# The sign of a 64-bit weight comes in with its scaling: windowed attention and two expert layers on one core

## Chip, cores and metric

One core of a Trainium2 chip. The metric is the device time of one execution in microseconds (us), as the median of several runs; the profile comes from one execution of its own.

## What is computed

Three stages follow one another: a windowed causal attention (4 sequences, 8 heads, 576 positions, 64 columns per head, window 128), an expert layer with a rational function, and an expert layer with an exponential unit. Cut to what matters:

```python
scores = where(mask, scale * q @ k.T - slope * abs(rel), -1e9)
x  = softmax(scores) @ v                       # 2304 tokens x 512
h  = x @ w_in                                  # 512 x 2048
g  = (a0 + a1*h + a2*h**2 + a3*h**3) / (1 + abs(b0)*abs(h) + abs(b1)*h**2 + 1e-6)
x  = g @ w_out                                 # 2048 x 512
h  = x @ w2_in
g  = where(h > 0, h, exp(min(h, 0)) - 1)
out = g @ w2_out
```

All four weight matrices arrive as 64-bit floats. The kernel makes 32-bit values of them on the chip, and splits each of these into a rounded part (type fp32r) and a rest, so that three matmuls of fp32r parts stand for one of full precision.

## The kernel before

**One weight word.** A 64-bit float lies in memory as a low and a high 32-bit word. Read as a 32-bit float, the high word has the right order of exponent bits, but three bits too far to the right. The kernel converts a tile of 128x512 words in four steps, named by letters: `s` (`conv_scale`, L126) multiplies the high words by 2^-112; `a` (`conv_shift`, L141) shifts the low words right by 29; `b` (`conv_or`, L144) shifts the scaled words left by 3, which pushes the sign out, and sets the three bits of `a`; `c` (`conv_sign`, L151) takes the sign bit of the high word by an "and" and sets it by an "or". Then `h` (`conv_hi`, L158) writes the rounded part over the place of the raw words, and `l` (`conv_lo`, L166) the rest. `s` writes into one of three rotating tiles (`cvt`), so the `s` of a tile waits until the `l` of the third tile before it has read.

**Attention.** 16 units (a sequence and a pair of heads) run as a software pipeline. Each iteration of its loop goes through the list `STEPS` (L18), which fixes by hand the order of the work on each engine; the number beside a step says of which unit, ahead or behind, it is the step. `T` are transposes of probabilities on TensorE, `C` their copies out of PSUM, `S` the scores, `D` the shifted scores with their maximum (VectorE, L503), `E` the exponentials with their sums (ScalarE, L518; each ends with a read of the accumulator), `R0` and `R1` the inverses of the sums (VectorE, L527 and L530), `N` the scaling of the probabilities by them (GpSimd, L535), `V` and `Y` the products with v, `XC` the copy of the result (ScalarE, L444, tile `xT`). `PLAN` (L32) puts the conversion of two weight tiles, numbered 0 and 1, into each of 12 units: steps `s0`, `s1`, `a0` and so on. `ENG` (L37) names the engine of a step: `s0` runs on GpSimd, `s1` on ScalarE, `h0` and `h1` on ScalarE, the rest of the conversion on VectorE. The order on the engines that matters below, within one iteration:

- ScalarE: `C01`, `C00`, `E6`, `E8`, `C10`, `C11`, `E1`, `E2`, `E4`, `E3`, `s1`, `E0`, `h1`, `E7`, `qC`, `h0`, `E5`, `XC`
- VectorE: `a0`, `l1`, `a1`, `D1`, `D3`, `l0`, `D2`, `D4`, `R1`, `b0`, `D0`, `kC`, `c0`, `D7`, `D5`, `D6`, `R0`, `b1`, `D8`, `c1`, `zC`, `XY`

Eight more tiles are converted around the end of the attention and in the first block of the rational layer by `conv_step` (L181), in the same steps.

**Rational layer.** 96 steps of 12 matmuls into `h` (L260) and 12 into `acc` (L708) alternate on TensorE; ScalarE and VectorE compute the rational function between them. Beside 54 of these steps half a tile of the next layer's weights is converted (`join_scale` on ScalarE, `join_shift`, `join_words`, `join_sign` on VectorE) and stored to DRAM by a transfer from the SP queue.

**Exponential layer.** A planner (`in_order`, L1127) puts all steps in order from a cost and a due time of each. Five weight tiles are still converted here (`scale_wo`, `join_wo`), with a planned cost of 1600 ns for the VectorE part.

Of the kernel before, what the change touches and what calls it, by code (L numbers as in the profile page):

```python
# [9 lines left out]
F32 = mybir.dt.float32  # L10
F32R = mybir.dt.float32r
I32 = mybir.dt.int32
# [24 lines left out]
ENG = {  # L37
    "h0": "A", "h1": "A", "s0": "G", "s1": "A", "l0": "D", "l1": "D", "qC": "A", "kC": "D",
    "zC": "D", "XC": "A", "XY": "D", "C00": "A", "C01": "A", "C10": "A", "C11": "A",
# [5 lines left out]
def kernel(  # L45
# [79 lines left out]

    def conv_scale(key, eng="A"):  # L126
        T32[key] = t = cv_tile([P, PC], F32, "cvt")
        high = words(key)[1].bitcast(F32)
        if eng == "G":
            nc.gpsimd.tensor_scalar(  # L130
                out=t, in0=high, scalar1=2.0 ** -112, scalar2=1.0, op0=ALU.mult, op1=ALU.mult
            )
        else:
            nc.scalar.activation(out=t, in_=high, func=AF.Copy, scale=2.0 ** -112)  # L134

# [8 lines left out]
    def conv_or(key):  # L144
        low, _ = words(key)
        ti = T32[key].bitcast(I32)
        nc.vector.scalar_tensor_tensor(
            out=ti, in0=ti, scalar=3, in1=low, op0=ALU.logical_shift_left, op1=ALU.bitwise_or
        )

    def conv_sign(key):  # L151
        _, high = words(key)
        ti = T32[key].bitcast(I32)
        nc.vector.scalar_tensor_tensor(
            out=ti, in0=high, scalar=-2147483648, in1=ti, op0=ALU.bitwise_and, op1=ALU.bitwise_or
        )
# [24 lines left out]
    def conv_step(keys, more=True, later=False):  # L181
        while put_off:
            go_on()
        if not (keys or stage["scaled"] or stage["whole"]):
            return
        new = keys.pop(0) if keys and more else None
        scaled, whole = stage["scaled"], stage["whole"]
        stage["scaled"], stage["whole"] = new, scaled
        if whole:
            conv_hi(whole)  # L190
        if new:
            conv_scale(new)
        if scaled:
            put_off.append(lambda: conv_shift(scaled))
            put_off.append(lambda: conv_or(scaled))
            put_off.append(lambda: conv_sign(scaled))
        if whole:
            put_off.append(lambda: conv_lo(whole, "D"))
        while put_off and not later:
            go_on()  # L200
# [124 lines left out]
    def attention():  # L325
        with ExitStack() as es:
# [280 lines left out]
            for e in range(2):  # L607
                RUN[f"V{e}"] = attn_v(e * NF // 2)
                for half in range(2):
                    RUN[f"T{e}{half}"] = probs_T(e, half)  # L610
                    RUN[f"C{e}{half}"] = probs_T_copy(e, half, ENG[f"C{e}{half}"])
            CONV = {"s": conv_scale, "a": conv_shift, "b": conv_or, "c": conv_sign, "h": conv_hi, "l": conv_lo}

# [82 lines left out]
    def experts():  # L696
# [71 lines left out]
        def join_scale(n):  # L768
            if n >= 2 * len(early_ones):
                return  # L770
            high = half[n].rearrange("p (c t) -> p c t", t=2)[:, :, 1]
            whole[n] = w = row("glo3" if n % 2 else "ghi3")[:, 0:HC]
            nc.scalar.activation(out=w, in_=high.bitcast(F32), func=AF.Copy, scale=2.0 ** -112)

# [9 lines left out]

        def join_sign(n):
            high = half.pop(n).rearrange("p (c t) -> p c t", t=2)[:, :, 1]
            w = whole.pop(n)
            wi = w.bitcast(I32)
            nc.vector.scalar_tensor_tensor(
                out=wi, in0=high, scalar=-2147483648, in1=wi, op0=ALU.bitwise_and, op1=ALU.bitwise_or  # L790
            )
            key = early_ones[n // 2]
            if n % 2 == 0:
                joined[key] = dram.tile([P, PC], F32, name="joined_%s_%d" % key)
            nc.sync.dma_start(out=joined[key][:, n % 2 * HC:(n % 2 + 1) * HC], in_=w)
# [27 lines left out]
        def scale_wo(q, e):  # L823
            key = ("wo", KF + 2 * q + e)
            T32[key] = both(e)
            nc.scalar.activation(out=both(e), in_=words(key)[1].bitcast(F32), func=AF.Copy, scale=2.0 ** -112)

        def join_wo(q, e):
            key = ("wo", KF + 2 * q + e)
            conv_shift(key)  # L830
            conv_or(key)
            conv_sign(key)
            del RAW[key]
# [204 lines left out]
        def weight_steps(w):  # L1038
# [22 lines left out]
            for e, x in enumerate("EF"):  # L1061
                gone = [(w - 2, "G", n) for n in ((0, 3), (1, 2))[e]]
                if e in raw_ones(w):
                    if w > 0:
                        step((w, "raw", x), "SP", 600, lambda e=e: load_raw(w, e), *gone)
                    step((w, "scale", x), "ACT", 570, lambda e=e: scale_wo(w, e), (w, "raw", x), (w - 1, "lo", x),
                         (w - 1, "keep", x))
                    step((w, "words", x), "DVE", 1600, lambda e=e: join_wo(w, e), (w, "scale", x))
                    step((w, "keep", x), "SP", 600, lambda e=e: keep_wo(w, e), (w, "words", x))
# [156 lines left out]
        for s in range(NCH):  # L1226
# [10 lines left out]
            if joins(s):  # L1237
                rational(s, beside=(lambda: join_shift(nj), lambda: join_words(nj), lambda: join_sign(nj)))
                nj += 1
# [50 lines left out]
```

## Time and profile before

| | |
|---|---|
| time, median of 3 runs | 941.23 us (939.8 to 941.63) |
| the profiled execution, first to last instruction | 939.7 us |
| busy: TensorE, VectorE, ScalarE, GpSimd | 920.0, 815.8, 745.7, 199.7 us |
| instructions | 16811 |

The span runs from the first to the last instruction of the program; the runs' times also hold what lies around it. In the rows below, PE is TensorE, PEld its weight loads, ACT is ScalarE, DVE is VectorE, POOL is GpSimd. An instruction of ACT or DVE can begin before the one ahead of it has ended, so its cost in a full queue is the distance between two starts, which is less than its duration. Shares of the whole span are averages over three stages with different limits.

### The profile page before, as it was taken

The page shows a single profiled execution, that of the slowest core. Times are in us where ns is not written, and L with a number is a line of the kernel's source. Part 1 is how long each engine was busy: PE and PEld are TensorE (multiplying, and loading weights), DVE is VectorE, ACT ScalarE, POOL GpSimd, SP SyncE. Part 2 cuts the span into 40 slices and gives each one's busy share as a digit, 9 for nine tenths or more (in the row PEclk, how much of TensorE's full clock was granted, in tenths as well). Part 3 has the DMA queues.
Part 4 walks back from the last instruction along what each step waited for, and adds up shares of the span by engine and source line. Part 5 has one row for each costly group of instructions (what it writes and reads, how often), then busy time and mean ns, then how long its engine had stood idle before and what let it go on. Part 6 is the DMA issues. An engine that isn't in the chain of part 4 may idle for free.

```text
span 939.7 us, 16811 instructions
## 1 busy us (share of the span) xinstructions
PE 920.0 (98%) x5494; PEld 840.3 (89%) x5494; DVE 815.8 (87%) x1930; ACT 745.7 (79%) x1635; POOL 199.7 (21%) x272
## 2 busy tenths in 40 slices
PE   8999989999999999999999999999999999999998
PEld 5776768999999999999999998888888888888887
DVE  6999998999999999999999999999968688777653
ACT  6999998889889889889888987576867567766553
POOL 5777772122222222222222220000000000000000
PEclk9999999999999999999999999999999999999999
DMA  9899942011231222222211043444353422442201
GB/s 192 226 227 229 235 129 90 1 34 35 85 98 55 85 84 68 84 70 85 80 45 34 1 135 112 149 145 159 109 169 113 123 79 90 157 146 80 79 0 68
DMA packets 112423, 98.35 MB, mean 105 GB/s; under 512 B 62800, under 2 KB 86096, under 8 KB 112336
## 3 DMA queue, kind: packets, MB, share of 16 engines
q1 hardware_dynamic: 109936, 96.70, 35.3%
q10 hardware_dynamic: 2400, 0.59, 0.4%
q8 instruction: 43, 0.70, 0.3%
q14 instruction: 44, 0.36, 0.1%
HBM read 79.96 MB, written 17.30 MB: 103 GB/s over the span
## 4 chain that ended last, share of the span: by engine, by line
PE 70%; ACT 13%; DVE 13%; issue 2%; DMA 1%; DVEq 0%; ACTq 0%; SPq 0%
PE acc L937 21%; PE m L921 18%; PE h L260 14%; PE acc L708 14%; ACT pT L444 2%; ACT pr_wi L518 2%; ACT pr_wo L518 2%; DVE ghi L301 2%; DVE qq L304 2%; DVE ee L322 1%; DVE ee L318 1%; DVE qq L313 1%; DVE h L321 1%; ACT cvt L134 1%; DMA k_wi<-in_k_dram 1%
## 5 line engine op out<-in xcount | busy, mean ns | idle before, releaser
L260 PE MATMUL h<-xs,w_wi 128*128 128x384 f32 x1152 | 218.2, 335 | 1.3 <-ACT xs L235 0.8
L260 PEld LDWEIGHTS h<-xs,w_wi 128*128 128x128 f32 x1152 | 200.5, 188 | 4.2 <-DVE xs L236 2.4
L708 PE MATMUL acc<-ghi,w_wo 128*128 128x384 f32 x768 | 194.9, 334 | 0.0
L319 POOL TENSOR_TENSOR glo<-ee,rr 128x384 fp32r<-128x384 f32 x92 | 93.4, 1015 | 316.4 <-DVE ee L318 161.0
L708 PEld LDWEIGHTS acc<-ghi,w_wo 128*128 128x128 f32 x768 | 138.6, 188 | 0.0
L708 PE MATMUL acc<-glo,w_wo 128*128 128x384 f32 x384 | 128.6, 335 | 0.4 <-POOL glo L319 0.2
L307 ACT ACTIVATE rr<-qq,c_q 128x384 f32<-128x384 f32 x96 | 59.2, 617 | 39.1 <-DVE qq L304 38.1
L937 PE MATMUL acc<-op_wo,ghi 128*128 128x512 f32 x288 | 89.6, 392 | 0.0
L921 PE MATMUL m<-xo_wo,op_wi 128*128 128x384 f32 x336 | 77.5, 339 | 2.3 <-DVE ee L977 2.3
L921 PE MATMUL m<-xo_wi,op_wi 128*128 128x384 f32 x336 | 77.8, 339 | 0.0
L708 PEld LDWEIGHTS acc<-glo,w_wo 128*128 128x128 f32 x384 | 72.1, 188 | 1.2 <-POOL glo L319 1.2
L290 ACT ACTIVATE oo<-h,a_sb 128x384 f32<-128x384 f32 x96 | 67.9, 707 | 4.4 <-DVE h L321 3.7
L983 ACT ACTIVATE oo<-qq 128x384 f32<-128x384 f32 x24 | 12.6, 525 | 72.7 <-DVE qq L977 72.7
L293 ACT ACTIVATE ee<-h,a_sb 128x384 f32<-128x384 f32 x96 | 67.6, 704 | 0.0
L921 PEld LDWEIGHTS m<-xo_wo,op_wi 128*128 128x128 f32 x336 | 61.6, 190 | 6.4 <-ACT oo L987 2.6
L301 DVE TENSOR_TENSOR ghi<-ee,rr 128x384 fp32r<-128x384 f32 x96 | 53.6, 559 | 12.2 <-ACT oo L290 0.5
L322 DVE TENSOR_TENSOR ee<-ee,h 128x384 f32<-128x384 f32 x96 | 53.3, 555 | 10.0
L937 PEld LDWEIGHTS acc<-op_wo,ghi 128*128 128x128 f32 x288 | 53.5, 188 | 8.9
L921 PEld LDWEIGHTS m<-xo_wi,op_wi 128*128 128x128 f32 x336 | 61.1, 189 | 0.0
L304 DVE SCALAR_TENSOR_TENSOR qq<-h,b_abs,qa 128x384 f32<-128x384 f32 x92 | 55.9, 608 | 3.7 <-ACT qa L289 3.7
L977 DVE TENSOR_TENSOR ee<-ee,m 128x384 f32<-128x384 f32 x96 | 52.6, 549 | 5.1 <-PE m L921 4.9
L937 PE MATMUL acc<-op_wo,glo 128*128 128x512 f32 x144 | 56.9, 395 | 0.0
(197 smaller groups left out, 2125.4 us busy)
## 6 DMA issues: line engine op xcount, KB each, us to landing
pair<-joined_wo SPq DMA_DIRECT2D x43, 256.0 KB, 2.7
raw_wo<-in_moe_w_out_dram SPq DMA_DIRECT2D x20, 512.0 KB, 5.1
raw_wi<-in_moe_w_in_dram SPq DMA_DIRECT2D x16, 512.0 KB, 4.5
half<-in_moe_w_in_dram SPq DMA_DIRECT2D x32, 256.0 KB, 2.8
two_wo<-joined_wi SPq DMA_DIRECT2D x32, 256.0 KB, 3.0
s<-sums SPq DMA_DIRECT2D x32, 256.0 KB, 2.8
half<-in_moe_w_out_dram SPq DMA_DIRECT2D x22, 256.0 KB, 2.8
v<-in_v_dram SPq DMA_DIRECT2D x32, 128.0 KB, 3.3
```

The costliest lines, as they stand in the source:

```text
L260: nc.tensor.matmul(h, lhsT=WT["wi", f][:, SEL[wp], kk * P:(kk + 1) * P], rhs=x[xp][kk], start=(kk == 0 and n == 0), stop=(kk == KD - 1 and ...
L290: nc.scalar.activation(out=oo, in_=h2, func=AF.Identity, scale=a_sb[:, 3:4], bias=a_sb[:, 1:2])
L293: nc.scalar.activation(out=ee, in_=h2, func=AF.Identity, scale=a_sb[:, 2:3], bias=a_sb[:, 0:1])
L301: nc.vector.tensor_tensor(out=hi, in0=ee0, in1=rr0, op=ALU.mult)
L304: nc.vector.scalar_tensor_tensor(out=qq, in0=h2, scalar=b_abs[:, 1:2], in1=qa, op0=ALU.mult, op1=ALU.add)
L307: nc.scalar.activation(out=rr, in_=qq, func=AF.Ln, bias=c_q)
L319: (nc.gpsimd if c > 4 else nc.vector).tensor_tensor(out=low, in0=ee0, in1=rr0, op=ALU.mult)
L322: nc.vector.tensor_tensor(out=ee, in0=ee, in1=h, op=ALU.add)
L708: nc.tensor.matmul(acc_t[d], lhsT=WT["wo", f][:, SEL[wp], d * P:(d + 1) * P], rhs=gt[SEL[xp]], start=(f == 0 and n == 0), stop=(f == KF - ...
L921: nc.tensor.matmul(out, lhsT=w[:, SEL[wp], c0:c0 + P], rhs=XO[q // NP2, nm, k][:, SEL[xp]], start=(k == 0 and n == 0), stop=(k == 1 and n ...
L937: nc.tensor.matmul(acc_t[T, t], lhsT=gt[SEL[xp]][:, t * P:(t + 1) * P], rhs=w[:, SEL[wp]], start=(first and n == 0), stop=(last and n == 2),)
L977: nc.vector.tensor_tensor(out=t, in0=R[q, x], in1=M[q, m], op=ALU.add)
```

## The change

The scaling becomes a Prelu, which multiplies a positive value by 1 and a negative one by a slope. With scale 2^-112 and slope 2^32, a negative value keeps one more exponent bit, which the shift left by 3 moves into the place of the sign. Step `c` goes away everywhere: 24 tiles in the attention, 8 by `conv_step`, 54 half tiles in the rational layer, 5 tiles in the exponential layer. In the attention `s0` moves from GpSimd to ScalarE, and `h0` and `h1` move from ScalarE to VectorE, at the same places of `STEPS`. The planner counts 950 ns in place of 1600 for the VectorE part of the last five tiles.

```diff
-    ("c0", 1), ("D7", 1), ("E4", 1), ("N7", 0), ("N8", 0), ("D5", 1), ("E3", 1),
+    ("D7", 1), ("E4", 1), ("N7", 0), ("N8", 0), ("D5", 1), ("E3", 1),
...
-    ("qT", 3), ("h1", 0), ("b1", 1), ("D8", 1), ("V1", -1), ("E7", 1), ("c1", 1),
+    ("qT", 3), ("h1", 0), ("b1", 1), ("D8", 1), ("V1", -1), ("E7", 1), 
...
-    "h0": "A", "h1": "A", "s0": "G", "s1": "A", "l0": "D", "l1": "D", "qC": "A", "kC": "D",
+    "h0": "D", "h1": "D", "l0": "D", "l1": "D", "qC": "A", "kC": "D",
...
+    def scale_words(out, high):
+
+        nc.scalar.activation(out=out, in_=high, func=AF.Prelu, scale=2.0 ** -112, alpha=2.0 ** 32)
...
-    def conv_sign(key):
-        _, high = words(key)
-        ti = T32[key].bitcast(I32)
-        nc.vector.scalar_tensor_tensor(
-            out=ti, in0=high, scalar=-2147483648, in1=ti, op0=ALU.bitwise_and, op1=ALU.bitwise_or
-        )
...
-            put_off.append(lambda: conv_sign(scaled))
...
-            nc.scalar.activation(out=w, in_=high.bitcast(F32), func=AF.Copy, scale=2.0 ** -112)
+            scale_words(w, high.bitcast(F32))
...
-                    step((w, "words", x), "DVE", 1600, lambda e=e: join_wo(w, e), (w, "scale", x))
+                    step((w, "words", x), "DVE", 950, lambda e=e: join_wo(w, e), (w, "scale", x))
...
-                rational(s, beside=(lambda: join_shift(nj), lambda: join_words(nj), lambda: join_sign(nj)))
+                rational(s, beside=(lambda: join_shift(nj), lambda: join_words(nj), lambda: keep_half(nj)))
```

`conv_scale` and `scale_wo` call `scale_words` too; `keep_half` is what was left of `join_sign`: the transfer to DRAM.

## Rows read from the trace of the kernel before

**Rows 1.** Stretch, length, busy PE, PEld, DVE, ACT, POOL, clock, DMA share, GB/s.
```profile
50.00:120.00 70.00, 66.61 (x663) 48.97 (x660) 69.46 (x266) 70.00 (x219) 54.27 (x81) 1.00 0.91 226
156.00:560.00 404.00, 402.55 (x2308) 399.47 (x2308) 376.12 (x810) 353.78 (x697) 93.36 (x92) 1.00 0.20 60
570.00:925.00 355.00, 355.00 (x1765) 319.51 (x1764) 283.73 (x559) 232.58 (x469) 0.00 (x0) 1.00 0.36 112
```

**Rows 2.** Chain that ended last, 82 to 120 us, shares by engine and line.
```profile
by line: ACT pT L444 21.8%; ACT pr_wo L518 20.2%; ACT pr_wi L518 16.6%; issue 14.0%; ACT cvt L134 7.6%; ACT rr L518 5.5%; ACT w_wi L164 5.3%; ACT qkT L444 5.1%; ACT w_wo L164 4.2%
```

**Rows 3.** ScalarE in order of time: start us, duration us, what; two iterations' ends.
```profile
35.86 0.58 ACT L444 ACTIVATE xT<-x 128x512 f32<-128x512 f32 x1
...
122.57 0.58 ACT L444 ACTIVATE xT<-x 128x512 f32<-128x512 f32 x1
```

**Rows 4.** ScalarE in order of time, one iteration: E8, s1, E0, h1, E7.
```profile
63.79 0.55 ACT L518 ACTIVATE pr_wo<-pr_wo,qq 128x256 f32<-128x256 f32 x1
...
66.99 0.73 ACT L134 ACTIVATE cvt<-raw_wo 128x512 f32<-128x512 f32 x1
67.56 0.50 ACT L518 ACTIVATE rr<-rr,qq 128x192 f32<-128x192 f32 x1
67.91 0.25 ACT L518 ACTIVATION_READ_ACCUMULATOR rr<-rr,qq 128x1 f32 x1
68.00 0.68 ACT L164 ACTIVATE w_wo<-cvt 128x512 fp32r<-128x512 f32 x1
68.52 0.55 ACT L518 ACTIVATE pr_wi<-pr_wi,qq 128x256 f32<-128x256 f32 x1
```

**Rows 5.** VectorE in order of time: R0, c1, zC, a0, l1.
```profile
60.28 0.24 DVE L527 TENSOR_SCALAR qq<-qq 128x5 f32<-128x5 f32 x1
...
61.57 0.69 DVE L154 SCALAR_TENSOR_TENSOR cvt<-raw_wo,cvt 128x512 int32<-128x512 int32 x1
62.17 0.28 DVE L446 COPY qkT<-ty 128x128 f32<-128x128 f32 x1
...
62.51 0.42 DVE L137 TENSOR_SCALAR raw_wi<-raw_wi 128x512 int32<-128x512 int32 x1
62.84 0.68 DVE L168 TENSOR_TENSOR w_wo<-cvt,w_wo 128x512 fp32r<-128x512 f32 x1
```

**Rows 6.** GpSimd in order of time: s0 and what it waited for.
```profile
63.61 0.79 POOL L130 TENSOR_SCALAR cvt<-raw_wi 128x512 f32<-128x512 f32 x1 [1.15 <-DVE w_wo L168]
```

**Rows 7.** VectorE groups by shape: busy us, mean ns of one, idle before them.
```profile
L446 DVE COPY qkT<-ps_qk 128x512 f32<-128x512 f32 x16 | 11.0, 685 | 0.0
L137 DVE TENSOR_SCALAR raw_wo<-raw_wo 128x512 int32<-128x512 int32 x20 | 8.4, 422 | 0.0
L789 DVE SCALAR_TENSOR_TENSOR glo<-half,glo 128x256 int32<-128x256 int32 x27 | 11.3, 418 | 0.0
```

**Rows 8.** ScalarE groups: busy us, mean ns of one, idle before them.
```profile
L307 ACT ACTIVATE rr<-qq,c_q 128x384 f32<-128x384 f32 x96 | 59.2, 617 | 39.1 <-DVE qq L304 38.1
L308 ACT ACTIVATE rr<-rr 128x384 f32<-128x384 f32 x96 | 50.5, 526 | 3.0
L638 ACT ACT_TABLE_LOAD x1 | 1.3, 1283 | 2.7 <-issue 2.7
```

**Rows 9.** ScalarE in order of time behind the attention's last conversions.
```profile
144.65 0.63 ACT L164 ACTIVATE w_wi<-cvt 128x512 fp32r<-128x512 f32 x1 [0.52 <-DVE cvt L154]
```

**Rows 10.** Chain that ended last, 160 to 214 us, shares by engine and line.
```profile
by line: DVE ghi L301 12.3%; DVE qq L304 11.8%; DVE ee L318 7.7%; DVE ee L322 7.4%; DVE h L321 7.2%; DVE qq L313 7.0%; ACT rr L307 5.6%; ACT oo L290 5.1%; ACT rr L308 4.9%; DVE cvt L154 4.5%; DVE cvt L147 4.5%; issue 3.8%; ACT cvt L134 3.5%
```

**Rows 11.** Waits of TensorE, 190 to 220 us: us in total, times, longest.
```profile
PE h L260 <- ACT xs L235: 0.5, 1, 0.5
PE h L260 <- DVE xs L236: 0.4, 1, 0.4
```

**Rows 12.** Wait of TensorE, 540 to 600 us.
```profile
PE m L921 <- DVE ee L977: 2.3, 1, 2.3
```

**Rows 13.** Chain that ended last, 478 to 565 us, shares by engine and line.
```profile
by line: DVE ghi L301 10.7%; DVE ee L322 9.8%; DVE qq L304 9.2%; DVE ee L318 7.8%; DVE qq L313 7.7%; DVE h L321 6.7%; issue 6.6%; ACT rr L307 3.5%; DVE xo_wi L878 3.3%; ACT rr L308 3.0%; DVE xo_wo L878 2.9%; DVE s L851 2.5%; ACT h L288 2.4%
```

More of the change, by code (lines that the diff above doesn't have):

```diff
@@ L124, in words, with conv_scale @@
         return raw[:, :, 0], raw[:, :, 1]
-    def conv_scale(key, eng="A"):
+    def scale_words(out, high):
+        nc.scalar.activation(out=out, in_=high, func=AF.Prelu, scale=2.0 ** -112, alpha=2.0 ** 32)
+    def conv_scale(key):
         T32[key] = t = cv_tile([P, PC], F32, "cvt")
         high = words(key)[1].bitcast(F32)
-        if eng == "G":
-            nc.gpsimd.tensor_scalar(
-                out=t, in0=high, scalar1=2.0 ** -112, scalar2=1.0, op0=ALU.mult, op1=ALU.mult
-            )
-        else:
-            nc.scalar.activation(out=t, in_=high, func=AF.Copy, scale=2.0 ** -112)
+        scale_words(t, high)
     def shift(low):
@@ L148, in conv_or @@
             out=ti, in0=ti, scalar=3, in1=low, op0=ALU.logical_shift_left, op1=ALU.bitwise_or
-        )
-    def conv_sign(key):
-        _, high = words(key)
-        ti = T32[key].bitcast(I32)
-        nc.vector.scalar_tensor_tensor(
-            out=ti, in0=high, scalar=-2147483648, in1=ti, op0=ALU.bitwise_and, op1=ALU.bitwise_or
         )
@@ L611, in attention @@
                     RUN[f"C{e}{half}"] = probs_T_copy(e, half, ENG[f"C{e}{half}"])
-            CONV = {"s": conv_scale, "a": conv_shift, "b": conv_or, "c": conv_sign, "h": conv_hi, "l": conv_lo}
+            CONV = {"s": conv_scale, "a": conv_shift, "b": conv_or, "h": conv_hi, "l": conv_lo}
             def run(step, u):
@@ L783, in join_words, with keep_half @@
             )
-        def join_sign(n):
-            high = half.pop(n).rearrange("p (c t) -> p c t", t=2)[:, :, 1]
+        def keep_half(n):
+            half.pop(n)
             w = whole.pop(n)
[L788 to L791, printed above, removed]
             key = early_ones[n // 2]
@@ L825, in scale_wo @@
             T32[key] = both(e)
-            nc.scalar.activation(out=both(e), in_=words(key)[1].bitcast(F32), func=AF.Copy, scale=2.0 ** -112)
+            scale_words(both(e), words(key)[1].bitcast(F32))
         def join_wo(q, e):
@@ L831, in join_wo @@
             conv_or(key)
-            conv_sign(key)
             del RAW[key]
```

## The prediction, made before the changed kernel was run

> **What bounds the kernel now.** I read the busy time by stage first, because the whole-span shares mix three stages. From 156 us to 560 us, the rational layer, TensorE is busy 402.55 of 404 us, and from 570 to 925 us, the exponential layer, 355.00 of 355 [rows 1]. There the other engines have room: ScalarE is busy 353.78 of 404 and 232.58 of 355. What the change takes off VectorE and ScalarE in these two stages is worth nothing, except at the few places where TensorE stands still. The attention is different: from 50 to 120 us ScalarE is busy 70.00 of 70 us and VectorE 69.46, TensorE 66.61 [rows 1]. The chain of waits in this stage has ScalarE instructions alone, and among them the scaling (7.6%) and the rounded parts (5.3% and 4.2%) that the change moves [rows 2]. So the change is worth what it takes off an iteration of the attention, times the iterations, and what it takes off TensorE's stalls later. When the attention ends earlier, all that follows begins earlier, since TensorE is full from there on.
>
> One iteration lasts (122.57 - 35.86) / 10 = 8.67 us, the copy `XC` from the one to the other ten iterations later [rows 3].
>
> **The attention, engine by engine.** On ScalarE the two `h` go: one costs 68.52 - 68.00 = 0.52 us from start to start, two 1.04. `s0` comes in, at the price of `s1`, 67.56 - 66.99 = 0.57 [rows 4]. ScalarE by itself would need 8.67 - 1.04 + 0.57 = 8.20 us. On VectorE the two `c` go, 62.17 - 61.57 = 0.60 each, and two copies of 128x512 from SBUF to SBUF come [rows 5]. No such copy stands in the trace. A bound from below is the shift, one input, the same size, both sides in SBUF: 422 ns long, and 62.84 - 62.51 = 0.33 from start to start [rows 5, 7]. A bound from above is a copy of the same size out of PSUM, 685 ns long, or `l1`, as long as `c`, so 0.60 from start to start [rows 5, 7]. I take 0.33, since the shift shares with the copy both the single input and the place of its data. The Trainium skill, "VectorE: DVE Perf Modes", section on the perf-mode tier table, says that 32-bit copies and tensor-scalar operations within SBUF run at two elements per cycle and that PSUM operands lose this; 422 against 685 ns agrees, and by that rule the copy comes out at the lower price too. VectorE by itself then needs 8.67 - 1.20 + 0.66 = 8.13 us. GpSimd loses `s0` (0.79 us) and the 1.15 us for which it stood in front of it [rows 6]; it was not on the chain, so this counts as nothing.
>
> **A new wait.** Neither 8.20 nor 8.13 is what I expect, because `s0` brings its wait along. GpSimd waited 1.15 us with it for `l1` [rows 6]: `s0` needs the rotating tile that `l1` frees. On ScalarE everything queues behind that wait, `E8` to `E0`, and `R0` on VectorE waits for `E0`, and `l1` comes behind `R0`. This is a ring through both engines, and its length is a lower limit of the iteration. ScalarE from `E8` to `E0`: 67.56 - 63.79 = 3.77, plus 0.57 for `s0`. `E0` with its accumulator read: 67.91 + 0.25 - 67.56 = 0.60 [rows 4]. VectorE from the start of `R0` to the end of `l1`: 62.84 + 0.68 - 60.28 = 3.24, less `c1` 0.60, plus the two copies 0.66 (both stand between `R0` and `l1`) = 3.30 [rows 5]. For each of the two passages from engine to engine 0.09, as `l1` ended at 63.52 and `s0` began at 63.61 [rows 5, 6]. The sum is 4.34 + 0.60 + 3.30 + 0.18 = 8.42 us. The ring is longer than either engine's own work, so it sets the iteration: 0.25 us less than now, in 12 iterations **3.0 us**. Before the change there was no such ring, as `s0` stood in a queue of its own.
>
> The price of the Prelu is the other unknown. From below it is that of the Copy that it replaces. From above: an operand that is read per partition costs 617 - 526 = 0.09 us more here, for two functions of otherwise equal size [rows 8]; if the slope were read so, `s0` and `s1` would each be dearer by 0.09. I take the lower, since scale and slope are both constants in the code.
>
> **The end of the attention.** One more `h` (0.52 us) leaves ScalarE in the iteration after the twelve. Behind it ScalarE stood 0.52 us for a sign step in front of a rounded part [rows 9]; in this `conv_step` the sign goes and the wait with it. Both lie on the chain that leads to TensorE's full stretch: **1.0 us**.
>
> **TensorE's stalls in the rational layer.** Between 156 and 560 us TensorE is idle for 404 - 402.55 = 1.45 us [rows 1], of which 0.9 us are waits for the split of the next block near 214 us [rows 11]. The chain up to there runs through VectorE, and sign steps are 4.5% of its 54 us, that is 2.4 us in four steps [rows 10]. This is more than the stalls are, so nearly all of them should go: **1.0 us**, between 0 and 1.3.
>
> **The change of layers.** Near 565 us TensorE waits 2.3 us for VectorE [rows 12], and the chain runs back through VectorE and ScalarE to 478 us [rows 13]. From 478 us on, three of the `join_sign` are left out, each 0.34 us from start to start (418 ns long [rows 7], with the overlap of 0.08 of the longer ones). That is 1.0 us if VectorE keeps the lead until 565 us and 0 if it only waits longer for TensorE in between: **0.5 us**.
>
> **What costs nothing.** The other 51 `join_sign` (0.34 us each, 17 us of VectorE) lie under TensorE's full queue, and so do the five `c` of the exponential layer; the planner's new cost can reorder steps there, under the same cover. If that cover were gone, a misplaced step would show as a wait of TensorE, of which there are none now between 570 and 925 us [rows 1]. The transfers behind `keep_half` stay at their place. The transfers of weights and of q, k and v come closer together in the attention (DMA share 0.91 there [rows 1]); an iteration 3% shorter asks for 3% more, and their first users come iterations later, so I count nothing.
>
> **Sum.** 3.0 + 1.0 + 1.0 + 0.5 = 5.5 us off the profiled span of 939.7 us. The median of the runs, 941.23, is 1.5 us above that span (what lies around it, and the scatter of runs); I take the difference off the median: 935.7 us.
>
> **Rivals.**
>
> - *The ring is not felt*, because VectorE reaches `l1` earlier than I think. Then ScalarE's own 8.20 us holds: 0.47 x 12 = 5.6 us, in all 8.1 off, 933.1 us; with all stalls gone 932.3. For it: ScalarE waits for nothing in this stage now. Against it: the ring's parts are all measured, and `E0` does stand in front of `R0`.
> - *The slope is read like a per-partition operand.* The ring is 8.60, the gain 0.07 x 12 = 0.8, in all 3.3 off: 937.9 us.
> - *The copy runs at the upper price*, 0.60 from start to start. The ring grows to 8.42 + 0.54 = 8.96 us, which is 0.29 more than now: 12 iterations lose 3.5 us, the other terms give 2.5 back, 942.2 us. With a copy above 0.46 us the attention becomes slower than it is. If the slope is dearer besides, 944.3.
> - *The Prelu is not in the table that is loaded*, so the change doesn't do what it says. The trace has one table load in all, of 1283 ns [rows 8], for every function used. A load in front of each scaling and one behind it would be 2.57 us. In the attention this is 24 x 2.57 = 62 us on the engine that is full. In the rational layer ScalarE is idle (404 - 353.78) us over the 96 steps of that layer, 0.52 per step, so each of 54 joins would cost 2.05 us, 111 in all: 941 + 173 - 5.5, about 1109 us. It decides as soon as the function is missing. The Trainium skill, "ScalarE: Activation LUTs", section on table sets, says that functions are loaded in named sets, that cheap functions are in every set, and that each switch of sets is paid; it names no Prelu in its list, and no row here has one. What speaks against this rival in the trace is that six different functions run behind the one load.
>
> **How the numbers follow.** Chances: the forecast 0.45, the ring not felt 0.15, the dearer slope 0.17, the dearer copy 0.13, the missing table entry 0.05, and 0.05 for a wait that I don't see and that eats the gain. 0.2% is 1.9 us, about what a measurement of this kernel can tell from no change. Faster by more: 0.45 + 0.15 + 0.17 = 0.77. Within it: most of the dearer copy and of the unseen wait, 0.12. Slower: the table, and the dearer copy with the dearer slope, 0.11. The forecast alone lies between 934 and 938 us. The range reaches from 932.3 (everything gained) to 940.5, which leaves out the dearer copy and the table.
>
> **What the profile after would show.** The distance of the `XC` copies should be 8.4 us, with ScalarE idle some 0.2 us in each iteration in front of `s0`, released by `l1`, and VectorE idle in front of `R0`. The copies on VectorE should last 0.42 us, the Prelu as long as the Copy before, 0.67 to 0.73. TensorE's waits near 214 us should be gone and the one near 565 us shorter. The prediction is wrong if the copies last 0.68, if there is more than one table load, or if the iteration is shorter than 8.3 us.

## The result, and the profile after

The changed kernel takes 933.23 us, median of 4 runs (933.09 to 933.9), against 941.05 us for the kernel before in the same session (4 runs, 939.8 to 941.63). The ratio is 0.9919, interval 0.9905 to 0.9933. The forecast was 935.7 us in a range of 932.3 to 940.5: the time is in the range, and the gain is 7.8 us where 5.5 were forecast. The profiled execution after took 933.09 us with a span of 931.4, which is 8.3 us shorter than the span before. Part of the 7.8 us is TensorE's clock, which fell to its lower level for 3.4 us at a time in some executions (below). Among the runs with a mean granted clock of 1.00, 17 of the kernel before have a median of 939.4 us, and the two of the changed kernel took 933.13 (here) and 932.1 (e13): about 6.8 us at equal clock.

Busy time by stage after, in the columns of [rows 1]:

```profile
50.00:120.00 70.00, 68.33 (x696) 51.16 (x697) 68.94 (x273) 69.07 (x218) 46.44 (x76) 1.00 0.95 228
150.00:550.00 400.00, 399.24 (x2299) 398.32 (x2300) 361.00 (x750) 354.49 (x697) 93.67 (x92) 1.00 0.19 61
560.00:917.00 357.00, 357.00 (x1772) 321.16 (x1772) 282.63 (x557) 233.49 (x470) 0.00 (x0) 1.00 0.34 112
```

In the attention VectorE (68.94) and ScalarE (69.07) are still nearly full, and TensorE has come up to 68.33. Later, TensorE is full as before.

ScalarE after, in order of time: two ends of an iteration, ten iterations apart [rows 3], and between them one turn of the ring [rows 4]. L128 is the scaling `s0` (it reads `raw_wi`), L509 with `rr` is `E0`:

```profile
34.62 0.59 ACT L435 ACTIVATE xT<-x 128x512 f32<-128x512 f32 x1
...
62.12 0.70 ACT L128 ACTIVATE cvt<-raw_wi 128x512 f32<-128x512 f32 x1
...
66.51 0.44 ACT L509 ACTIVATE rr<-rr,qq 128x192 f32<-128x192 f32 x1
66.86 0.19 ACT L509 ACTIVATION_READ_ACCUMULATOR rr<-rr,qq 128x1 f32 x1
...
70.24 0.19 ACT L509 ACTIVATION_READ_ACCUMULATOR pr_wo<-pr_wo,qq 128x1 f32 x1
70.55 0.70 ACT L128 ACTIVATE cvt<-raw_wi 128x512 f32<-128x512 f32 x1
...
119.03 0.58 ACT L435 ACTIVATE xT<-x 128x512 f32<-128x512 f32 x1
```

An iteration lasts (119.03 - 34.62) / 10 = 8.44 us, against 8.67 before; the forecast was 8.42. Ahead of the second `s0`, ScalarE stands idle from about 70.33 (a read of the accumulator costs 0.09 from start to start) to 70.55: 0.22 us, the wait that the prediction expected there.

VectorE in the same iteration [rows 5]: `R0` (L518), the new copies `h1` and `h0` (L154, listed as CAST), `a0` (L136, `raw_wi`), `l1` (L160, `w_wo`), `a1` (L136, `raw_wo`) and the step behind it:

```profile
67.07 0.32 DVE L518 TENSOR_SCALAR qq<-qq 128x5 f32<-128x5 f32 x1
67.43 0.19 DVE L521 RECIPROCAL qq<-qq 128x5 f32<-128x5 f32 x1
67.54 0.39 DVE L154 CAST w_wo<-cvt 128x512 fp32r<-128x512 f32 x1
67.84 0.69 DVE L146 SCALAR_TENSOR_TENSOR cvt<-cvt,raw_wo 128x512 int32<-128x512 int32 x1
...
68.99 0.42 DVE L154 CAST w_wi<-cvt 128x512 fp32r<-128x512 f32 x1
69.32 0.22 DVE L437 COPY xT<-ty 128x64 f32<-128x64 f32 x1
69.45 0.48 DVE L136 TENSOR_SCALAR raw_wi<-raw_wi 128x512 int32<-128x512 int32 x1
69.85 0.67 DVE L160 TENSOR_TENSOR w_wo<-cvt,w_wo 128x512 fp32r<-128x512 f32 x1
70.44 0.63 DVE L136 TENSOR_SCALAR raw_wo<-raw_wo 128x512 int32<-128x512 int32 x1
70.99 0.27 DVE L494 CUSTOM_DVE_ANT_0 pr_wi<-s_ps,h 128x128 f32<-128x128 f32 x1
```

The copies cost 67.84 - 67.54 = 0.30 and 69.32 - 68.99 = 0.33, as forecast. But the shifts have grown: `a1` costs 70.99 - 70.44 = 0.55 and `a0` 69.85 - 69.45 = 0.40, where a shift cost 0.33 before, and `R0` costs 67.43 - 67.07 = 0.36, where it cost 0.27 (60.55 - 60.28 in the trace before). No idle time stands in front of `R0`, where the prediction expected some. GpSimd beside it [rows 6]:

```profile
66.44 0.93 POOL L526 TENSOR_SCALAR pr_wo<-pr_wo,qq 128x256 f32<-128x256 f32 x2
...
69.62 1.16 POOL L526 TENSOR_SCALAR pr_wi<-pr_wi,qq 128x256 f32<-128x256 f32 x1
```

Its work ends at 66.44 + 0.93 = 67.37, and `R0` ends at 67.39. Its instruction from 69.62 ends at 70.78, and `a1`, begun at 70.44, lets the next step start 0.21 us after that. `s0` has left GpSimd, and its other work now falls beside these steps. In the kernel before `R0` ended at 60.52 [rows 5], and GpSimd beside it at 60.49:

```profile
60.02 0.47 POOL L535 TENSOR_SCALAR pr_wo<-pr_wo,qq 128x256 f32<-128x256 f32 x1
```

So `R0` already ended with a GpSimd instruction there, 0.07 us later than where it is free (0.17 long in e10).

Groups over the whole span (busy us, mean ns of one, idle before) [rows 7, 8]:

```profile
L154 DVE CAST w_wi<-cvt 128x512 fp32r<-128x512 f32 x12 | 5.0, 418 | 0.0
L136 DVE TENSOR_SCALAR raw_wo<-raw_wo 128x512 int32<-128x512 int32 x20 | 10.5, 527 | 0.0
L128 ACT ACTIVATE cvt<-raw_wi 128x512 f32<-128x512 f32 x16 | 11.1, 693 | 0.8
L629 ACT ACT_TABLE_LOAD x1 | 1.3, 1283 | 2.7 <-issue 2.7
```

There is one table load, as before. The Prelu lasts 693 ns, in the band that was given for it (0.67 to 0.73). The copy lasts 418 ns, and the shift has gone from 422 to 527 in the mean.

TensorE's waits from 140 to 560 us [rows 11, 12]:

```profile
PE m L907 <- DVE ee L963: 2.3, 1, 2.3
PE ps_pT L542 <- ACT pT L435: 1.4, 1, 1.4
```

The waits for `xs` near 214 us are gone. The wait at the change of layers is 2.3 us, as before.

From the two traces, between instructions that both have:

| stretch | before | after | gained | forecast |
|---|---|---|---|---|
| start to the first `XC` copy | 27.11 | 26.06 | 1.05 | 0 |
| twelve iterations of the attention, 1st to 13th `XC` | 103.68 | 100.93 | 2.75 | 3.0 |
| end of the attention, to TensorE's `h` at 162.14 (157.05 after) | 31.35 | 30.06 | 1.29 | 1.0 |
| first block of the rational layer, to `acc` at 216.66 (209.29) | 54.52 | 52.24 | 2.28 | 1.0 with the next row |
| the other blocks, to `acc` at 551.09 (542.62) | 334.43 | 333.33 | 1.10 | |
| change of layers and exponential layer, to the last `m` | 374.33 | 374.48 | -0.15 | 0.5 |

The rest to the end is 14.3 us in both. The sum is 8.3 us.

In the first and the third row the two executions differ in TensorE's clock, too, and in the last row it fell in both. The kernel before, in three stretches (columns as above):

```profile
16.00:18.00 2.00, 2.00 (x12) 1.23 (x9) 1.49 (x7) 1.93 (x10) 1.28 (x3) 0.50 0.67 154
151.60:155.00 3.40, 3.40 (x28) 3.00 (x28) 2.85 (x6) 3.16 (x8) 0.00 (x0) 0.50 0.49 158
564.70:567.90 3.20, 2.94 (x9) 2.97 (x10) 2.72 (x6) 2.29 (x6) 0.00 (x0) 0.50 0.29 76
```

The changed kernel at the start and behind the change of layers:

```profile
16.00:18.00 2.00, 1.93 (x16) 1.32 (x15) 1.97 (x12) 2.00 (x9) 1.41 (x4) 1.00 0.74 162
557.50:560.50 3.00, 3.00 (x10) 2.91 (x10) 1.85 (x4) 2.77 (x7) 0.00 (x0) 0.50 0.00 1
```

And a second execution of the changed kernel (e13) behind the change of layers:

```profile
557.50:560.50 3.00, 3.00 (x17) 2.78 (x16) 3.00 (x6) 3.00 (x8) 0.00 (x0) 1.00 0.06 23
```

The granted clock was 0.50, the lower of its two levels, three times in that execution of the kernel before, once in that of the changed kernel, and never from the start to the end of e13. The later falls came at the end of a stop of TensorE or within 0.9 us behind it: 2.1 us long until 151.23 in the kernel before, 2.3 us at the change of layers in both. The same stop of 2.2 to 2.3 us stands in all 14 profiled executions, and the clock fell there in five of them: before, after, e1, e5 and e10. What each fall cost:

- Start: the first `XC` comes at 25.7 to 26.6 us in the other profiles (26.02 in e13), except in e6 (27.36, where TensorE waits for q), so about 1 us of the first row belongs to that execution of the kernel before. This is inferred, not tested.
- End of the attention: the last interval of `XC` is 8.00 us before and 7.64 to 7.66 in every other profile, with and without sign steps. So 0.35 of the 1.29 us is the clock, and 0.94 the change.
- Exponential layer: the last row takes 374.3 to 374.5 us where the clock fell (before, after, e5), 372.9 in e13. The fall costs 1.5 us, and it hits both kernels of the table alike.

### The profile page after: what moved, and what is told of

Read it like the earlier page. It is cut to its first block, busy times and chain, and to the rows that moved or that the text cites. A ratio compares the mean times of both kernels' runs of the same rounds, so it can differ in the third digit from the quotient of the medians.

```text
span 931.4 us, 16710 instructions
## 1 busy us (share of the span) xinstructions
PE 913.8 (98%) x5494; PEld 838.8 (90%) x5494; DVE 792.0 (85%) x1863; ACT 741.9 (80%) x1623; POOL 185.2 (20%) x260
## 4 chain that ended last, share of the span: by engine, by line
PE 79%; DVE 14%; ACT 3%; DMA 2%; issue 1%; DVEq 0%; ACTq 0%; SPq 0%
PE acc L923 21%; PE m L907 18%; PE acc L699 18%; PE h L251 18%; DVE pr_wi L494 2%; DVE pr_wo L494 1%; DVE cvt L146 1%; PE s_ps L468 1%; DVE qkT L437 1%; DVE ghi L292 1%; PE x L561 1%; DVE ee L313 1%; DMA q_wo<-in_q_dram 1%; PE ps_pT L542 1%; DVE w_wi L160 1%
## 5 line engine op out<-in xcount | busy, mean ns | idle before, releaser
L279 ACT ACTIVATE h<-h 128x384 f32<-128x384 f32 x96 | 46.3, 483 | 14.8 <-PE h L251 14.2
```

## The experiments

All but e6 are edits of the changed kernel, e6 is one of the kernel before. Their ratios are to the kernel before on the same chip, with which they alternated (the medians of the kernel before: 940.25 us beside e1 to e4, 940.88 beside e6, e7, e9 and e10, 939.52 beside e5 and e11 to e13).

**e1, open the ring.** `s0` goes behind `C10` in `STEPS`, so that ScalarE has `l1`'s release before it gets there.

```diff
-    ... ("T10", -1), ("s0", 1), ("D1", 1), ...
+    ... ("T10", -1), ("D1", 1), ...
-    ... ("R1", 0), ("b0", 1), ...
+    ... ("R1", 0), ("s0", 1), ("b0", 1), ...
```

> The changed kernel with the scaling of tile 0 (s0) put after C10 in the list of steps, so that ScalarE reaches it long after l1 has freed its tile; nothing else differs. Theory (the ring s0, E0, R0, l1 sets the iteration of 8.44 us): the ring shrinks by E8 and C10, about 0.97 us, so it no longer sets the end; the iteration falls to ScalarE's own 8.20 to 8.25 us, ScalarE no longer waits in front of s0, and the time is 12 x 0.2 = 2.4 us under the changed kernel's 933.2: 930.8. Rival (the iteration is set by something else, VectorE held up by GpSimd or TensorE): the iteration stays within 0.05 of 8.44 us and the time within 0.6 of 933.2.

Measured: 933.52 us, 0.9925 (0.9903 to 0.9947), the same as the changed kernel. The steady iteration stays at 8.43 to 8.45 us, so the rival holds. `R0` now begins 0.26 us after the end of `E0` (0.02 in the changed kernel), and `s0` 0.76 us after `l1` (0.03): the ring is open. VectorE and GpSimd of e1 in order of time:

```profile
75.10 1.39 POOL L526 TENSOR_SCALAR pr_wo<-pr_wo,qq 128x256 f32<-128x256 f32 x3
...
76.15 0.37 DVE L518 TENSOR_SCALAR qq<-qq 128x5 f32<-128x5 f32 x1
...
79.56 0.63 DVE L136 TENSOR_SCALAR raw_wo<-raw_wo 128x512 int32<-128x512 int32 x1
```

`R0` again ends with GpSimd's work (76.52 and 76.49), `a1` is as long as in the changed kernel, and VectorE has no idle time from 60 to 118 us. So the ring is not alone in setting 8.44: with it open, VectorE by itself is just as long.

**e10, the shift `a1` behind `D3`**, where GpSimd has finished; `s0` stays in its place.

```diff
-    ("a1", 1), ("E6", 0), ("T10", -1), ("s0", 1), ("D1", 1), ("D3", 1), ("E8", 0),
+    ("E6", 0), ("T10", -1), ("s0", 1), ("D1", 1), ("D3", 1), ("a1", 1), ("E8", 0),
```

> The changed kernel with only the shift a1 moved behind D3; s0 stays where the change has it. It tells whether the ring through ScalarE is a limit of its own at 8.4 us beside VectorE's work, since a1 does not lie between R0 and l1. If the ring is a limit: the iteration stays at 8.4 to 8.44 us, VectorE stands idle about 0.2 us in front of R0 in each iteration and ScalarE in front of s0, 933 us. If VectorE's work alone is one: 8.23 us and 931, as with both steps moved.

Measured: 931.42 us, 0.9902 (0.9887 to 0.9917); the iteration is 8.26 to 8.29 us. VectorE of e10 in order of time, `R0`, `l1` and `a1`:

```profile
66.65 0.17 DVE L518 TENSOR_SCALAR qq<-qq 128x5 f32<-128x5 f32 x1 [0.16 <-ACT rr L509]
...
69.27 0.67 DVE L160 TENSOR_TENSOR w_wo<-cvt,w_wo 128x512 fp32r<-128x512 f32 x1
...
70.42 0.42 DVE L136 TENSOR_SCALAR raw_wo<-raw_wo 128x512 int32<-128x512 int32 x1
70.75 0.68 DVE L160 TENSOR_TENSOR w_wi<-cvt,w_wi 128x512 fp32r<-128x512 f32 x1
```

`a1` is back at 70.75 - 70.42 = 0.33, `R0` at 0.17 long, and now VectorE does wait 0.16 us for `E0`. This is the ring of the prediction, at 8.28 us. Neither expectation came whole: the idle time in front of `R0` is there, as for a ring that is the limit, but the ring is shorter than 8.4, since `R0` now begins 0.10 us before GpSimd's work ends and costs 0.20 (66.85 - 66.65) in place of 0.36. The stretch from `R0` to the end of `l1` is 69.27 + 0.67 - 66.65 = 3.29 us (3.30 forecast).

**e9, both moves together.**

```diff
-    ("a1", 1), ("E6", 0), ("T10", -1), ("s0", 1), ("D1", 1), ("D3", 1), ("E8", 0),
+    ("E6", 0), ("T10", -1), ("D1", 1), ("D3", 1), ("a1", 1), ("E8", 0),
-    ... ("R1", 0), ("b0", 1), ...
+    ... ("R1", 0), ("s0", 1), ("b0", 1), ...
```

> The changed kernel with two steps moved in the list: s0 behind C10 (as in the run before this one, which opened the ring and left the iteration at 8.44 us) and the shift a1 behind D3, a place at which GpSimd is idle. Theory now (VectorE's own work is the limit, and it is 0.3 us longer than I added up, because a1 takes 0.55 us from start to start in place of 0.33 while GpSimd works beside it): a1 takes 0.33 again, the iteration is 8.23 us, the time about 931. Rival (the iteration hangs on something that neither the ring nor the shift touches, such as TensorE): 8.44 us, 933.2.

Measured: 931.71 us, 0.9909 (0.9891 to 0.9927). The iterations from the fifth to the ninth last 8.17 to 8.19 us, the 8.20 that the prediction gave for ScalarE by itself; ScalarE has no idle time from 60 to 112 us. The next two last 8.24 and 8.25, as `R0` comes to lie beside GpSimd's work again (0.37 long). The median is no better than that of e10, as two early iterations last 8.88 and 9.22 us: TensorE waits there twice in front of a matmul into `ps_qk`, 2.3 us together. So e1, e10 and e9 together show two limits of equal length in the changed kernel, 8.44 us each: VectorE's own work, and the ring, which is 8.28 without the hold of `R0`. ScalarE's own work lies below them, and so does TensorE's, which kept up with 8.17.

**e11, `a0` moved as well** (`a0` and `a1` behind `D3`, `s0` behind `C10`).

```diff
-    ("T00", -1), ("a0", 1), ("l1", -1), ...
-    ("a1", 1), ("E6", 0), ("T10", -1), ("s0", 1), ("D1", 1), ("D3", 1), ("E8", 0),
+    ("T00", -1), ("l1", -1), ...
+    ("E6", 0), ("T10", -1), ("D1", 1), ("D3", 1), ("a0", 1), ("a1", 1), ("E8", 0),
-    ... ("R1", 0), ("b0", 1), ...
+    ... ("R1", 0), ("s0", 1), ("b0", 1), ...
```

> The changed kernel with both shifts (a0, a1) behind D3, where GpSimd is idle, and s0 behind C10. Theory (after the ring is open and the shifts are not held, ScalarE's own work is the last limit of the attention): the iteration is 8.18 to 8.20 us as with a1 and s0 moved, since ScalarE needs that; no gain from a0; 931. Rival (VectorE is still the limit): 0.06 us less per iteration, 8.12 us.

Measured: 932.29 us, 0.9912 (0.9896 to 0.9927), and a steady iteration of 8.31 to 8.35 us, longer than that of e9, which no theory expected. VectorE of e11 in order of time:

```profile
69.22 0.73 DVE L160 TENSOR_TENSOR w_wo<-cvt,w_wo 128x512 fp32r<-128x512 f32 x1
69.96 0.29 DVE L494 CUSTOM_DVE_ANT_0 pr_wi<-s_ps,h 128x128 f32<-128x128 f32 x1
```

`l1` now costs 0.74 us in place of 0.60. It has moved up against a GpSimd instruction that runs from 68.83 to 69.41. `R0` ends with GpSimd's work again, too (0.36 long). With the 0.14 us of `l1` VectorE has no room left, which would explain the 0.15 us between e11 and e9; this is read off the trace and not tested.

**e12, e11 with the loads of the weights behind those of q and k** in each iteration. **e13** is the changed kernel again, beside it on the same chip.

```diff
+                            if 2 <= u < 14:
+                                load_some(2)
...
-                if 0 <= t < 12:
-                    load_some(2)
```

> As the run with both shifts and s0 later, and the loads of the two weight tiles of an iteration are issued behind those of q and k rather than at the start of the iteration. With a shorter iteration TensorE waits in the third and fourth iteration for q to land (1.1 and 1.2 us in the run with a1 and s0 moved). Theory (the weights in front of q in the queue make it late): these waits go, 1.3 us less than without, about 929.8. Rival (the transfers are at their limit there, so another one is late): no change, within 0.5 us of the run without.

> The changed kernel itself, beside the others on the same chip: 933.2, iteration 8.44 us, shift a1 0.55 us from start to start. It also shows whether the first 27 us of the profile, which are 1.05 us shorter than before, repeat: theory (before had a lower clock from 14 to 20 us by chance): the copy XC of the first unit at 26.0 to 26.3 us.

Measured: e12 930.05 us, 0.9895 (0.9878 to 0.9912), the lowest median of all, though its interval overlaps those of e9 to e11; e13 933.19 us, 0.9926 (0.991 to 0.9943). TensorE's waits from 34 to 60 us in e13:

```profile
PE ps_qk L412 <- DMA q_wo<-in_q_dram: 1.2, 1, 1.2
PE ps_qk L412 <- DMA q_wi<-in_q_dram: 1.2, 1, 1.2
```

The first profile of the changed kernel has such a wait from 34 to 60 us, too, and the kernel before has none from 20 to 60 us:

```profile
PE ps_qk L412 <- DMA q_wo<-in_q_dram: 0.6, 1, 0.6
```

In e12 there are none for q. Its third to fifth iterations last 8.16 to 8.21 us, those of e11 8.34 to 8.56; later ones are equal (8.31 to 8.35). So late loads of q cost the changed kernel something, too: in e13 the third iteration lasts 9.1 us, in the first profile 8.56. At a granted clock of 1.00 the medians are 929.88 (e12, three runs) and 931.16 (e11, three runs), a gain of 1.3 us, as its theory said.

**e4, the dearer copy.** `h` in the attention is the maximum of the tile with itself, two inputs in place of one, with an equal value.

```diff
-            nc.vector.tensor_copy(w[:, 0], T32[key])
+            nc.vector.tensor_tensor(out=w[:, 0], in0=T32[key], in1=T32[key], op=ALU.max)
```

> The changed kernel with the rounded parts in the attention made by a maximum of the tile with itself in place of a copy: same values, but two inputs, so about 0.60 us from start to start in place of 0.33 and 0.30. This is the price that the rival of the dearer copy had. Theory (ring): both stand in the ring, which grows from 8.44 to 9.0 us; 12 iterations give 6.8 us, 940. Rival (ScalarE alone is the limit, and VectorE has the room): VectorE needs 8.7 us by itself, so the iteration would be 8.7 us and the time 936.3.

Measured: 938.37 us, 0.9973 (0.9961 to 0.9986). ScalarE of e4, the same two copies `XC`:

```profile
34.58 0.59 ACT L435 ACTIVATE xT<-x 128x512 f32<-128x512 f32 x1
...
123.46 0.57 ACT L435 ACTIVATE xT<-x 128x512 f32<-128x512 f32 x1
```

The distance is 8.89 us in the mean and 8.95 to 9.02 in the steady iterations, 0.54 more than 8.44: the two copies are paid in full. This is what the rival with the dearer copy forecast (8.96). The rival of the experiment, with ScalarE as the only limit, is out (8.7). The experiment does not tell the ring from a full VectorE, since the copies lie in both.

**e6, the engines without the Prelu.** The kernel before with `s0` on ScalarE and `h` on VectorE, and all sign steps kept.

```diff
-    "h0": "A", "h1": "A", "s0": "G", "s1": "A", "l0": "D", ...
+    "h0": "D", "h1": "D", "s0": "A", "s1": "A", "l0": "D", ...
```

> The kernel before with the moves between engines alone: h0 and h1 on VectorE, s0 on ScalarE as a Copy, and the sign step kept everywhere. Theory (in the attention the slower of VectorE and ScalarE sets the iteration): VectorE gains two copies of 0.33 on 8.67, so 9.3 us, and with the shift held by GpSimd up to 9.6; 12 iterations cost 8 to 11 us, 949 to 952. Rival (ScalarE is the limit before, VectorE has room): ScalarE's 0.47 us less make it faster, 936 to 940.

Measured: 949.83 us, 1.0105 (1.0085 to 1.0125), 9 us slower than before. Waits of e6 from 50 to 120 us:

```profile
ACT cvt L134 <- DVE w_wo L168: 7.7, 6, 1.3
```

From the fourth on, an iteration lasts 8.71 to 10.54 us, mostly 9.6, close to 8.44 + 2 x 0.60 for the two sign steps. The two of 10.5 hold the stretches from 78.7 and from 126.5 us in which the granted clock was 0.50. `s0` on ScalarE waits up to 1.3 us for `l1`, as forecast for the ring.

**e7, the Prelu without the engines.** Where the scaling ran on ScalarE it is a Prelu without a sign step; `s0` stays on GpSimd with its `c0`, and `h` on ScalarE.

```diff
-    "h0": "D", "h1": "D", "l0": "D", ...
+    "h0": "A", "h1": "A", "s0": "G", "l0": "D", ...
+    ("c0", 1), ("D7", 1), ...
```

> The Prelu and no sign step wherever the scaling was on ScalarE already (tile 1 in the attention, the conversions behind it, the rational and the exponential layer); in the attention s0 stays on GpSimd with its sign step c0, and h0 and h1 stay on ScalarE. Theory: ScalarE's work in an iteration is unchanged, so the attention stays at 8.65 to 8.67 us although VectorE loses 0.6 us; the gain is that of the later stages alone, 0.75 + 2.3 + 1.3 us, 936 to 937. Rival (VectorE alone was the limit before): the iteration falls to 8.1 to 8.4 us and the time to 933 or less.

Measured: 934.72 us, 0.9943 (0.9928 to 0.9957). The attention gains nothing, 8.65 us an iteration, and VectorE waits in it. The view of waits of e7, VectorE from 50 to 120 us:

```profile
DVE qq L530 <- ACT pr_wo L521: 2.0, 7, 0.3
DVE qq L530 <- ACT rr L521: 1.7, 7, 0.2
```

What e7 gains comes later: its first block of the rational layer takes 52.22 us, as after. So in the attention neither half of the change gains alone; the sign steps have to go for VectorE to have room for `h`, and `h` has to leave ScalarE.

**e3, the sign step back in the eight tiles of `conv_step`.** It sets a bit that the Prelu has already set, so it is work and nothing else; the same holds for e2.

```diff
+            put_off.append(lambda: conv_sign(scaled))
```

> The changed kernel with the sign step put back in the eight conversions around the end of the attention and in the first block of the rational layer, same result. Theory (the chain through VectorE sets these stretches): about 1 us at the end of the attention and about 2.3 us in the first block come back, 936.5. Rival (the first block gains for another reason, such as the clock or the earlier end of the attention): less than 1 us, 933.2 to 934.2, and the distance between TensorE's first full group of the first block and its end stays at the changed kernel's.

Measured: 935.35 us, 0.9947 (0.993 to 0.9964). The first block takes 54.54 us, as before the change (54.52), and the waits of TensorE are back. The view of waits of e3 from 120 to 917 us:

```profile
PE h L259 <- ACT xs L234: 0.5, 1, 0.5
PE h L259 <- DVE xs L235: 0.4, 1, 0.4
```

From the twelfth `XC` to TensorE's `h` at 151.40 e3 takes 31.61 us, the changed kernel 30.85 (`h` at 149.88): 0.76 us of the end of the attention are the sign, too.

**e2, the sign step back in the 54 joins.**

```diff
+            nc.vector.scalar_tensor_tensor(
+                out=wi, in0=high, scalar=-2147483648, in1=wi, op0=ALU.bitwise_and, op1=ALU.bitwise_or
+            )
```

> The changed kernel with the sign step put back on VectorE beside the 54 half tiles of the rational layer (it sets again the bit that is already there, so the result is the same). Theory of the prediction (all but the last three lie under TensorE's full queue): within 0.5 us of 933.2. Rival, from the comparison of the two profiles (from the second block of the rational layer on, TensorE's groups come 1.25 us earlier than at its beginning, in four jumps of 0.3 at the block borders): the jumps go, 934.4. If VectorE were the limit throughout, 54 x 0.34 = 18 us more.

Measured: 933.61 us, 0.9922 (0.9906 to 0.9939). The first block stays at 52.23 us. The blocks behind it take 334.74 us against 333.33, 1.4 us more, in steps at each border between blocks. TensorE of e2 at the first of them:

```profile
273.27 2.55 PE L251 MATMUL h<-xs,w_wi 128*128 128x384 f32 x12
275.67 0.33 PE L699 MATMUL acc<-ghi,w_wo 128*128 128x384 f32 x1
```

The changed kernel at the same place:

```profile
273.77 2.24 PE L251 MATMUL h<-xs,w_wi 128*128 128x384 f32 x12
275.85 0.33 PE L699 MATMUL acc<-ghi,w_wo 128*128 128x384 f32 x1
```

And the kernel before:

```profile
281.14 2.55 PE L260 MATMUL h<-xs,w_wi 128*128 128x384 f32 x12
283.52 0.33 PE L708 MATMUL acc<-ghi,w_wo 128*128 128x384 f32 x1
```

Twelve matmuls and the passage to the next take 2.40 us, 2.08 and 2.38. TensorE was late by 0.3 us there with the sign step, and no row of waits says so. In the median this 1.4 us hardly shows (933.61 against 933.23). In the profiled execution of e2 two stretches that the edit does not touch are shorter than in that of the changed kernel. The exponential layer is shorter by 1.5 us, which is the fall of the clock that e2 did not have. The attention up to the twelfth `XC` is shorter by 0.5 us; e2 has no wait for q from 20 to 60 us.

**e5, the planner's cost back at 1600 ns.**

```diff
-                    step((w, "words", x), "DVE", 950, ...
+                    step((w, "words", x), "DVE", 1600, ...
```

> The changed kernel with the planner's cost of the last five conversions back at 1600 ns. Theory (TensorE's queue covers whatever the planner reorders in the exponential layer): no wait of TensorE between 570 and 920 us, and the distance from the layer's start to its end is the same to 0.3 us apart from the clock. Rival (the honest cost moved steps of VectorE to better places): up to 0.5 us slower behind 560 us.

Measured: 931.61 us, 0.991 (0.9895 to 0.9926), 1.6 us below e13. From `acc` at the change of layers to the last `m` it takes 374.39 us, the changed kernel 374.48; the clock fell behind the change of layers in both. So the stage that the planner orders is the same to 0.1 us, as the theory said. e13 needs only 372.92 there, without the fall. The 1.6 us come from elsewhere: between the profiles of e13 and e5, 0.9 us lie in the early iterations of the attention, where the plan is the same, and four of the six runs of e5 have a granted clock of 1.00, one of the six of e13. The new cost buys nothing that these runs show.

## Why the prediction came out as it did

**The parts that held.** The copy costs 0.30 to 0.33 us; I took 0.33 between 0.33 and 0.60, and e4 shows that the upper end would have cost what the rival said. The Prelu costs what the Copy cost, and the table is loaded once (1283 ns). By the section on table sets of the Trainium skill's "ScalarE: Activation LUTs", a function outside the loaded set would have cost loads; the trace agrees that this one is inside, since there is one load in all. The end of the attention gave 0.94 at equal clock for the forecast 1.0: e3 finds 0.76 for the sign, and against e7, where `h` is still on ScalarE, the stretch is 0.31 shorter (30.37 and 30.06); the two together are a little more than the whole.

**The attention: a right sum out of two errors.** 8.42 us were forecast for the ring and 8.44 measured. Term by term, the ring after is 66.51 - 62.12 = 4.39 from `s0` to `E0`, 0.54 for `E0` with its read, 0.02 to `R0`, 70.52 - 67.07 = 3.45 from `R0` to the end of `l1`, and 0.03 to `s0`: 8.43. My passages (0.18 together, now 0.05) and `E0` (0.60) were too long. The way from `s0` to `E0` (4.34) and the stretch from `R0` to `l1` (3.30) were too short, the latter because `R0` lasts until GpSimd's instruction beside it ends, and `a0` is held as well. Without that hold the ring is 8.28, which e10 shows. The step that failed is the sum for VectorE by itself, "8.67 - 1.20 + 0.66 = 8.13 us". VectorE needs 8.44, because `a1` (0.21 us more), `R0` (0.09) and `a0` (0.07) are held beside GpSimd's instructions; `R1`, which cost 0.28 before, costs 0.19 and gives back 0.09. These four make 8.41. I took the start-to-start costs of before over as if they were the instructions' own, and counted `s0` leaving GpSimd "as nothing", though it shifted the rest of GpSimd's work against VectorE's. That VectorE so held is a limit is shown by e1 (ring open, nothing gained) and e10 (`a1` moved, 0.16 us an iteration gained).

**The rational layer: the mis-sized term.** "This is more than the stalls are, so nearly all of them should go: 1.0 us" measured 3.4: 2.28 in the first block and 1.10 at the later borders. The mechanism was right, and e3 and e2 show it apart: the eight sign steps of `conv_step` cost 2.3 us, those of the joins 1.4. The size was wrong because I capped it by TensorE's idle time, 1.45 us [rows 1, 11]. The ends of the matmuls in the profile are modelled, and part of the lateness hides in stretches that look busy: a group of twelve in 2.38 us in place of 2.08. The other bound that stood in the prediction, 2.4 us of sign steps on the chain [rows 10], was the better size for the first block. And "The other 51 `join_sign` lie under TensorE's full queue" was wrong at the borders between blocks, where e2 finds 1.4 us.

**The change of layers.** 0.5 us were forecast, nothing came: the wait is 2.3 us before and after [rows 12]. The lower of the two cases given there holds, that VectorE only waits longer in between: in the 87 us that end with TensorE's wait it is busy 81.74 us before (478 to 565) and 79.51 after (469.5 to 556.5), so the steps left out became idle time.

**The transfers.** Counted as nothing. Late loads of q cost e13 an iteration of 9.1 us and the first profile of the changed kernel a wait of 0.6 us, where the kernel before had none, and e12 gains 1.3 us over e11 at equal clock by their order. So the assumption was wrong, by a size that varies from execution to execution.

**The sum.** At equal clock the runs gain about 6.8 us, and the stages of the two profiles 6.9 (8.3 less 1.05 and 0.35), where 5.5 were forecast. The rational layer gave 2.4 us more than its 1.0, the twelve iterations 0.25 less than their 3.0, the change of layers nothing of its 0.5. The total was forecast 1.4 us too small, because of the rational layer; the misses in the attention and at the change of layers hide part of that.

## What to carry to other kernels

When two engines are full, add up both from start to start and also every ring of waits through them, and ask of each short step which engine ran beside it when it was measured: a step that leaves a third engine moves that engine's work against everyone else's. A stall of TensorE is not bounded by its idle time in the trace; compare the distance of equal groups of matmuls (2.08 us undisturbed here) at the places where something new must be ready. Before two profiles are compared stage by stage, the granted clock of each stage has to be compared: one fall of 3.4 us was worth up to 1.5 us here. A change that frees room on one engine and one that fills it can each be worth nothing or less alone (0.9943 with nothing gained in the attention, and 1.0105) and 0.9919 together.

## What was not expected of the hardware

A VectorE instruction with one input in SBUF can be held by GpSimd. A shift of 128x512 costs 0.33 us from start to start where GpSimd is idle (e10) and 0.55 where it runs into a GpSimd instruction of 1.16 us. `R0`, five numbers per partition, lasts 0.17 us where it is free, and otherwise until 0.02 to 0.04 us after the end of a GpSimd instruction: 0.24 before, 0.32 to 0.34 after, 0.36 to 0.38 in e1. The GpSimd instruction of 128x256 itself lasts 0.47 us at one place (before, 60.02) and 1.16 at another (after, 69.62), so the hold may go both ways; that VectorE is the cause there was not tested. The Trainium skill, "SBUF — State Buffer", section "Who interferes with whom", says that GpSimd and VectorE share a port pair which is held for a whole instruction, and that copies and tensor-scalar operations of VectorE can need it. The end of `R0` at 67.39 behind that of GpSimd at 67.37 agrees. Moving one shift behind two other steps of VectorE in a hand-written order was worth 0.16 us in every iteration.
